# Two ScalarE steps' scores in one visit to TensorE's row mode, an eighth pooled PSUM bank, and stage rules dropped, in an attention and feed-forward kernel

## The chip, the cores and the metric

The kernel runs on one core of one Trainium2 chip. The metric is the device time of one execution in microseconds (us); the span in a profile is some 1.8 us shorter (703.6 us for a run of 705.39). The core's engines are called here by the profile's names: PE is TensorE (PEld its weight loads), ACT is ScalarE, DVE is VectorE, POOL is GpSimd, SP is SyncE, which issues DMAs. The kernel's PSUM tile, `ps`, has eight banks; a bank holds one 128 x 512 tile in float32.

## The reference, cut to what matters

```
xn  = layernorm(x)                       # x: 2048 x 640
q   = xn @ wq  -> 32 heads of 20         # k, v: one head of 20 for all
p   = softmax(q k^T / sqrt(20))          # 32 x 2048 x 2048 scores
att = (p v) @ wo
ffn = relu(xn @ w1 + b1)**2 @ w2 + b2    # 640 -> 1536 -> 640
out = x + att + ffn
```

The scores are the bulk: 2048 tiles of 128 x 512, each of which needs an exponential.

## The kernel before

The program is not written down instruction by instruction. A list scheduler inside the kernel runs at build time: it keeps a clock for each engine and always takes next the operation that can start first, with priorities for ties. The order in which it takes them is the program. The parts that the change touches are these.

ACT takes two or three score tiles at a time from adjacent PSUM banks (a *step*). TensorE makes a score tile with 20 contracted rows, so four heads sit in four row tiles of the array; nearly everything else it does here uses column tiles of 32 columns.

```
def make_act(st_):
    n, s0, b0 = len(st_["tiles"]), st_["s0"], st_["banks"][0]
    ...
    return Op(f"ACT{st_['j']}", "ACT", 0.05 + 0.4267 * n, [... func=AF.Exp, bias=-EXP_SHIFT, scale=SCALE ...], deps)
```

DVE and POOL make the other exponentials in sets of four tiles from integer operations: DVE takes each score tile out of PSUM (`tmore<-ps`), then DVE or POOL makes three more passes over the set. When a step's scores are issued, free row tiles are filled with score tiles for DVE:

```
elif kind == "qk":
    take_step(ap[1])
    heads = [t[2] for t in ap[1]["tiles"]]
    while len(heads) < HPG:
        r = make_dqk(heads)            # a tile for DVE, if a bank is free
        ...
```

The product with V (called PV) of one block of queries accumulates in a bank of its own, number 7, over 16 key tiles, and is then copied out by DVE. The other seven banks form a pool for ACT's steps, DVE's tiles and the feed-forward and projection groups. Finally, the scheduler has some twenty parameters, and a table that changes them by *stage* (a stage is 10 us of ACT's time):

```
NB = 7            # pooled banks
PVB = 7           # PV's bank
RULES = {3: {'PVA': 2.1, 'PVD': 2.1, 'R3': 1, 'PP': 0.9},
         4: {'PVA': 2.1, 'PVD': 2.1, 'R3': 1, 'PP': 0.9, 'WARM': 0.78},
         ...                           # 70 stages in all, many with none
         69: {'R3': 0, 'JIT': 1.1}}
```

The softmax here doesn't subtract the row's maximum and nothing guards it: scores larger than these inputs give would overflow.

Of the kernel before, what the change touches and what calls it, by code (L numbers as in the profile page):

```python
# [25 lines left out]
EPS = 1e-5  # L26
# [9 lines left out]
def _pl(z):  # L36
# [9 lines left out]
NB = 7  # L46
PVB = 7
# [33 lines left out]
RULES = {3: {'PVA': 2.1, 'PVD': 2.1, 'R3': 1, 'PP': 0.9},  # L81
         4: {'PVA': 2.1, 'PVD': 2.1, 'R3': 1, 'PP': 0.9, 'WARM': 0.78},
         5: {'D1P': 1, 'MPRIO': 0.5, 'PBIAS': 2.5},
         6: {'D1P': 1, 'MPRIO': 0.5, 'PBIAS': 2.5, 'ND': 1, 'QKP': 0},
         7: {'DQP': 2.05, 'URG': 2, 'PVD': 2.1, 'BEHIND': -0.3},
         8: {'WARM': 0.85, 'DQP': 0.95},
         10: {'ND': 1, 'NOPEN': 3},
         11: {'ND': 1, 'NOPEN': 3},
         12: {'EPS': 0.12},
         13: {'EPS': 0.06, 'EVP': 0.3},  # L90
         15: {'PBIAS': 0},
         17: {'EPS': 0.06},
         18: {'EPS': 0.12},
         19: {'WARM': 0.78, 'PBIAS': 2.5, 'IDLE': 0.3},
         21: {'PBIAS': 0, 'KEEP': 0},
         23: {'EPS': 0.12},
         25: {'R3': 1, 'EVP': 0.3},
         26: {'R3': 1, 'EVP': 0.3, 'IDLE': 0.3, 'PVD': 2.1},
         28: {'EPS': 0.12, 'URG': 3},
         29: {'EPS': 0.12, 'URG': 3, 'KEEP': 3, 'EVP': 1.1, 'ND': 3},  # L100
         31: {'PBIAS': 1, 'D1P': 1, 'PVD': 1.05},
         32: {'PBIAS': 1, 'D1P': 1, 'PVD': 1.05, 'DGAP': 0.8, 'DQP': 0.95, 'SQP': 2, 'R3': 1},
         36: {'PP': 0.9, 'BEHIND': -0.1, 'EVP': 0.3, 'PBIAS': 1.5},
         37: {'URG': 3, 'JIT': 1.0, 'PVD': 1},
         38: {'SQP': 0.7, 'URG': 3},
         39: {'PP': 2.5},
         40: {'PBIAS': 1},
         41: {'PBIAS': 1, 'DGAP': 1.5, 'SQP': 0.7},
         42: {'PBIAS': 1, 'DGAP': 1.5, 'SQP': 2, 'NOPEN': 3, 'ND': 2, 'PVD': 1},
         43: {'PBIAS': 1, 'DGAP': 1.5, 'SQP': 2, 'NOPEN': 3, 'ND': 2, 'PVD': 1, 'R3': 9},  # L110
         44: {'WARM': 0.78, 'KEEP': 3, 'DLAST': 7.5},
         45: {'DGAP': 0.8, 'KEEP': 1, 'D1P': 3},
         48: {'PBIAS': 1},
         49: {'PBIAS': 1, 'R3': 1},
         50: {'PBIAS': 1, 'R3': 1},
         53: {'DLAST': 3.5},
         54: {'DLAST': 3.5, 'EPS': 0, 'EVP': 0.3},
         55: {'DLAST': 3.5, 'EPS': 0, 'EVP': 0.3, 'ND': 1},
         56: {'EVP': 2, 'MPRIO': 1.0},
         57: {'R3': 1, 'ND': 1},  # L120
         58: {'BEHIND': -0.1, 'EPS': 0, 'PP': 4, 'R3': 1},
         59: {'BEHIND': -0.1, 'EPS': 0, 'PP': 4, 'R3': 1, 'DRATE': 0.95, 'DLAST': 10, 'PVA': 2.1},
         60: {'EVP': 1.1},
         61: {'EVP': 1.1, 'SQP': 0.7},
         62: {'EVP': 1.1, 'SQP': 0.7, 'KEEP': 3, 'R3': 1, 'NOPEN': 2, 'D1P': 3},
         64: {'PP': 0.9, 'DRATE': 0.8},
         65: {'R3': 1},
         66: {'R3': 1},
         67: {'EPS': 0.12, 'PVA': 1.05},
         68: {'R3': 0},  # L130
         69: {'R3': 0, 'JIT': 1.1}}
HOOK = None
PRIO = {'NM15': 2.12, 'NM10': 2.88, 'PW2': 0.96}
NBEF = {'AG4': 10.21, 'NM7': 11.5, 'Qe0_1': 10.11, 'PW12': 25.33}
XACT = (1, 3)
QEACT = (0, 1, 2, 3)
STOP = None
WINDOW = 3.4
MPRIO = 0.9
BEHIND = 0.12  # L140
IDLE = 0.3
EARLY = 12
EARLYK = "F"
FFN0 = 0.3
OUT0 = 0.5
QLEAD = 3.0
PEND = NBLK - 3.0
QCPOS = 0
# [76 lines left out]
def bass_parallel_sum__grouped_kv_mqa__dense_activation_squared_relu__prompt_kernel(nc, A_x, A_wq, A_wk, A_wv, A_wo, B_x, B_w1, B_b1, B_w2, B_b2, out):  # L225
    es = ExitStack()
    with es:  # L227
# [694 lines left out]
        def make_pv(b, kt):  # L922
# [7 lines left out]
            if first and b > 0:  # L930
                deps.append(tn_op[b - 1])
# [527 lines left out]
```

## Time and profile before

| of the kernel before | |
|---|---|
| time, median of 4 runs | 705.88 us (705.3 to 706.61) |
| span; granted TensorE clock | 703.6 us; 1.00 |
| busy: PE, ACT, DVE, POOL | 99%, 98%, 92%, 61% |
| first exponential starts, last one ends | 15.30 us, 695.14 us |
| ACT's waits for PE in the exponentials | 3.8 us in 3 waits |

Read the table with the chain of waits, not with the busy shares. The chain lies on ACT's exponentials for 94% of the span, so the time is when the exponentials start, how much work they are, how long ACT stands still among them, and what follows the last. I use these four terms. All are read from the trace: the work is the count of steps times 0.490, 0.917 or 1.344 us for one, two or three tiles, and a stall is what lies between the ends of two successive steps beyond that price. Before, they are 15.30 + 677.0 + 2.7 + 8.50 = 703.5 us. The lines themselves stand in the prediction. Three words recur. The *ramp* is the start, up to about 40 us, the *tail* what follows the last exponential, and a *waiting step* is one whose scores must wait until the step just in front has been read, because it needs a bank of that step. In the lines, `PT<-ps` is an exponential of ACT, `ps<-qT,kT` scores, `tmore<-ps` a tile taken by DVE, `ps<-kT,zeros` filler matmuls whose result changes nothing, and `R<-drs` the small DMA that brings row sums.

### The profile page before, as it was taken

Reading aid. Unit: us, or ns where it says so; the run is one execution under the profiler, and the core shown is the slowest. Engines: PE = TensorE matmul, PEld = TensorE weight load, DVE = VectorE, ACT = ScalarE, POOL = GpSimd, SP = SyncE. Lnnn points to the kernel's source line nnn. Section 1 sums busy time; section 2 is a strip of 40 time slices with the busy share of each in tenths; the row PEclk is TensorE's granted clock in tenths of the full one; section 3 lists DMA queues with packets and bytes.
Section 4 is the critical chain, followed back from the end, with each engine's and each line's share of the span. In section 5 each row is a group of like instructions: output and inputs, shape, how many; then the busy total and the mean of one; then the engine's idle time right before and its main releaser. Section 6 shows DMA issues by size and latency. Waiting matters only on the chain.

```text
span 703.6 us, 22608 instructions
## 1 busy us (share of the span) xinstructions
PE 695.0 (99%) x9780; PEld 216.0 (31%) x9781; DVE 645.9 (92%) x1125; ACT 687.5 (98%) x739; POOL 427.3 (61%) x268
## 2 busy tenths in 40 slices
PE   8999999999999999999999999999999999999997
PEld 4422223233322223332322222323333222233333
DVE  7789999999999998989998998899899999999894
ACT  6899999999999999999999999999999999999995
POOL 4767556567566764666568765766665675644253
PEclk9999999999999999999999999999999999999999
DMA  6325422233337701211101001111112100031201
GB/s 201 98 70 153 115 78 58 81 97 80 84 85 160 162 20 25 55 40 37 52 18 40 23 22 28 29 47 26 46 42 51 36 22 23 20 106 51 55 26 39
DMA packets 42016, 44.00 MB, mean 63 GB/s; under 512 B 15540, under 2 KB 32772, under 8 KB 41788
## 3 DMA queue, kind: packets, MB, share of 16 engines
q1 hardware_dynamic: 39132, 36.93, 19.2%
q0 software_dynamic: 2208, 5.25, 3.9%
q8 instruction: 76, 1.25, 0.7%
q10 hardware_dynamic: 576, 0.38, 0.2%
q14 instruction: 24, 0.20, 0.1%
HBM read 28.03 MB, written 14.91 MB: 61 GB/s over the span
## 4 chain that ended last, share of the span: by engine, by line
ACT 95%; PE 4%; DMA 1%; DVE 0%; SPq 0%; issue 0%; DVEq 0%
ACT PT L910 94%; PE ps L367 3%; DMA x_sb<-in_A_x_dram 1%; PE ps L540 1%; ACT xnT L477 0%; ACT OC L421 0%; DVE out_sb L1164 0%; PE ps L568 0%; SPq L384 0%; ACT OC L422 0%; SPq L391 0%; PE ps L510 0%; PE ps L496 0%; DVEq L227 0%; DVE PT L1164 0%
## 5 line engine op out<-in xcount | busy, mean ns | idle before, releaser
L910 ACT ACTIVATE PT<-ps 128x1024 bf16<-128x1024 f32 (+1 forms) x715 | 677.1, 1219 | 3.8 <-PE ps L367 3.8
L1083 DVE TENSOR_SCALAR tmore<-ps 128x512 uint16<-128x512 f32 x568 | 367.4, 683 | 31.7 <-PE ps L367 28.2
L1101 POOL TENSOR_SCALAR tmore<-tmore 128x2048 uint16<-128x2048 uint16 x109 | 206.4, 1900 | 171.1 <-PE ps L367 62.3
L367 PE MATMUL ps<-qT,kT 20*128 20x512 bf16 x2048 | 281.7, 384 | 1.9 <-ACT PT L910 0.8
L1101 POOL TENSOR_SCALAR x_sb<-tmore 128x2048 uint16<-128x2048 uint16 x100 | 189.3, 1902 | 79.4 <-DVE x_sb L1101 24.2
L367 PEld LDWEIGHTS ps<-qT,kT 20*128 20x128 bf16 x2048 | 71.6, 91 | 280.4 <-ACT PT L910 233.1
L367 PE MATMUL ps<-PT,vx 128*32 128x512 bf16 x1480 | 136.9, 386 | 0.2 <-ACT PT L910 0.2
L1101 DVE TENSOR_SCALAR x_sb<-tmore 128x2048 uint16<-128x2048 uint16 x135 | 96.1, 745 | 0.1
L367 PE MATMUL ps<-x_sb,vxs 128*32 128x512 bf16 x940 | 83.2, 382 | 0.0
L367 PE MATMUL ps<-xnT,w_sb 128*32 128x512 bf16 x960 | 77.2, 384 | 0.1
L367 PE MATMUL ps<-w_sb,big 128*32 128x320 bf16 x1536 | 74.5, 302 | 0.0
L367 PE MATMUL ps<-tmore,vxs 128*32 128x512 bf16 x764 | 69.6, 382 | 0.0
L1101 DVE TENSOR_SCALAR tmore<-tmore 128x2048 uint16<-128x2048 uint16 x82 | 61.5, 770 | 0.1
L367 PE MATMUL ps<-tmore,vx 128*32 128x512 bf16 x568 | 55.7, 382 | 0.0
L367 PEld LDWEIGHTS ps<-PT,vx 128*32 128x32 bf16 x1480 | 34.9, 94 | 62.1 <-issue 53.6
L367 PEld LDWEIGHTS ps<-w_sb,big 128*32 128x32 bf16 x1536 | 32.1, 95 | 29.3 <-issue 22.2
L648 DVE TENSOR_SCALAR hT_tmp<-ps,b1col 128x512 bf16<-128x512 f32 x48 | 35.8, 746 | 3.4 <-PE ps L367 2.7
L367 PE MATMUL ps<-xnT,wq_sb 128*32 128x512 bf16 (+1 forms) x480 | 33.7, 356 | 0.2 <-DVE tmore L1083 0.2
L367 PE MATMUL ps<-wo_c,OC 128*32 128x320 bf16 x608 | 30.9, 301 | 0.0
L367 PEld LDWEIGHTS ps<-x_sb,vxs 128*32 128x32 bf16 x940 | 21.3, 95 | 19.9 <-issue 13.4
L367 PEld LDWEIGHTS ps<-xnT,w_sb 128*32 128x32 bf16 x960 | 17.6, 94 | 26.7 <-issue 22.4
L367 PEld LDWEIGHTS ps<-tmore,vxs 128*32 128x32 bf16 x764 | 18.1, 95 | 16.4 <-issue 11.5
(81 smaller groups left out, 259.4 us busy)
## 6 DMA issues: line engine op xcount, KB each, us to landing
xbd<-b2d SPq DMA_DIRECT2D x16, 320.0 KB, 4.4
xbd<-in_A_x_dram POOLq DMA_DIRECT2D x8, 640.0 KB, 5.8
xr<-xbd SPq DMA_DIRECT2D x32, 160.0 KB, 2.4
w_sb<-in_B_w_dram SPq DMA_DIRECT2D x8, 480.0 KB, 4.4
big<-OR SPq DMA_DIRECT2D x71, 40.0 KB
big<-drs SPq DMA_DIRECT2D x71, 40.0 KB
out_dram<-out_sb SPq DMA_DIRECT2D x15, 160.0 KB, 1.8
qT<-QCr SPq DMA_DIRECT2D x108, 20.0 KB
```

The costliest lines, as they stand in the source:

```text
L367: return lambda e: e.matmul(out_, l, r, start=start, stop=stop, tile_position=tp)
L540: return [(lambda e, dt=dt: e.transpose(out=psbf(bk)[:, dt * 128:(dt + 1) * 128], in_=xn_sb[:, st, dt:D:DT], identity=ident[:])) for dt in ...
L648: o = Op(f"RL{qc}_{f}", "DVE", 0.66, [lambda e: e.tensor_scalar(out=hT_tmp[:, k % 2, :], in0=ps[:, bk, :], scalar1=b1col[:, f:f + 1], scal ...
L910: return Op(f"ACT{st_['j']}", "ACT", 0.05 + 0.4267 * n, [lambda e: e.activation(out=PT[:, s0:s0 + n, :], in_=ps[:, b0:b0 + (n - 1) * db + ...
L1083: d1 = op(f"D1_{n}_{i}", "DVE", 0.60, lambda e: e.tensor_scalar(out=L[:, cs].bitcast(U16), in0=ps[:, bank, :], scalar1=XA, scalar2=XB, op0 ...
L1101: p = op(f"P{j}_{n}", eng, 0.60 if eng == "DVE" else 1.86, lambda e, T=T, j=j, two=two: e.tensor_scalar(out=T.bitcast(U16), in0=L.bitcast( ...
```

## The change

The intent is to spare TensorE some of its changes between row and column mode: if three pooled banks are still free after the scores of one step have been issued, the scores of the next step follow in the same visit. To have the banks, all eight are pooled, and PV takes whichever is free when a block begins. The table of rules is emptied, and a few settings change. `DJIT`, a new limit on how far ahead DVE's tiles are issued, plays no part: built with the limit at 99, the changed kernel is the same program.

```diff
-NB = 7
-PVB = 7
+NB = 8
+PV0 = 7
-RULES = {3: {'PVA': 2.1, 'PVD': 2.1, 'R3': 1, 'PP': 0.9},
- ... (70 stages)
+DJIT = 9.0
+DV = 3
+RULES = {}
-PRIO = {'NM15': 2.12, 'NM10': 2.88, 'PW2': 0.96}
-NBEF = {'AG4': 10.21, 'NM7': 11.5, 'Qe0_1': 10.11, 'PW12': 25.33}
+PRIO = {'XN1': 0.13}
+NBEF = {'S4a': 6.0, 'AG5': 10.23, 'PW1': 4.94}
-QEACT = (0, 1, 2, 3)
+QEACT = (0, 1)
-FFN0 = 0.3
+FFN0 = 0.6
 ... (ACTST and POOLXN: which engine does which row statistics)
+        def bank_for(b):
+            if b in pv_bank:
+                return pv_bank[b]
+            can = [(bank_state(bk), -bk) for bk in range(NB) if bank_state(bk) is not None and ...]
+            return -min(can)[1] if can else None
 ... (PV's matmuls and its copy use this bank; the copy frees it)
                 take_step(ap[1])
                 heads = [t[2] for t in ap[1]["tiles"]]
+                if len(heads) == 2 and ... sum(1 for bk in POOLED if bank_state(bk) is not None and bank_state(bk) <= o.start + 0.06) >= par("DV"):
+                    can = [bk for bk in range(NB - 1) if all(k != kept() and ... for k in (bk, bk + 1))]
+                    st_ = build_step(len(steps), [can[0], can[0] + 1], 0.0) if can else None
+                    ... (if its heads differ and it is ready: commit it, take it)
```

More of the change, by code (lines that the diff above doesn't have):

```diff
@@ L80 @@
 KEEP = 1
-RULES = {3: {'PVA': 2.1, 'PVD': 2.1, 'R3': 1, 'PP': 0.9},
-         4: {'PVA': 2.1, 'PVD': 2.1, 'R3': 1, 'PP': 0.9, 'WARM': 0.78},
-         5: {'D1P': 1, 'MPRIO': 0.5, 'PBIAS': 2.5},
-         6: {'D1P': 1, 'MPRIO': 0.5, 'PBIAS': 2.5, 'ND': 1, 'QKP': 0},
-         7: {'DQP': 2.05, 'URG': 2, 'PVD': 2.1, 'BEHIND': -0.3},
-         8: {'WARM': 0.85, 'DQP': 0.95},
-         10: {'ND': 1, 'NOPEN': 3},
-         11: {'ND': 1, 'NOPEN': 3},
-         12: {'EPS': 0.12},
-         13: {'EPS': 0.06, 'EVP': 0.3},
-         15: {'PBIAS': 0},
-         17: {'EPS': 0.06},
-         18: {'EPS': 0.12},
-         19: {'WARM': 0.78, 'PBIAS': 2.5, 'IDLE': 0.3},
-         21: {'PBIAS': 0, 'KEEP': 0},
-         23: {'EPS': 0.12},
-         25: {'R3': 1, 'EVP': 0.3},
-         26: {'R3': 1, 'EVP': 0.3, 'IDLE': 0.3, 'PVD': 2.1},
-         28: {'EPS': 0.12, 'URG': 3},
-         29: {'EPS': 0.12, 'URG': 3, 'KEEP': 3, 'EVP': 1.1, 'ND': 3},
-         31: {'PBIAS': 1, 'D1P': 1, 'PVD': 1.05},
-         32: {'PBIAS': 1, 'D1P': 1, 'PVD': 1.05, 'DGAP': 0.8, 'DQP': 0.95, 'SQP': 2, 'R3': 1},
-         36: {'PP': 0.9, 'BEHIND': -0.1, 'EVP': 0.3, 'PBIAS': 1.5},
-         37: {'URG': 3, 'JIT': 1.0, 'PVD': 1},
-         38: {'SQP': 0.7, 'URG': 3},
-         39: {'PP': 2.5},
-         40: {'PBIAS': 1},
-         41: {'PBIAS': 1, 'DGAP': 1.5, 'SQP': 0.7},
-         42: {'PBIAS': 1, 'DGAP': 1.5, 'SQP': 2, 'NOPEN': 3, 'ND': 2, 'PVD': 1},
-         43: {'PBIAS': 1, 'DGAP': 1.5, 'SQP': 2, 'NOPEN': 3, 'ND': 2, 'PVD': 1, 'R3': 9},
-         44: {'WARM': 0.78, 'KEEP': 3, 'DLAST': 7.5},
-         45: {'DGAP': 0.8, 'KEEP': 1, 'D1P': 3},
-         48: {'PBIAS': 1},
-         49: {'PBIAS': 1, 'R3': 1},
-         50: {'PBIAS': 1, 'R3': 1},
-         53: {'DLAST': 3.5},
-         54: {'DLAST': 3.5, 'EPS': 0, 'EVP': 0.3},
-         55: {'DLAST': 3.5, 'EPS': 0, 'EVP': 0.3, 'ND': 1},
-         56: {'EVP': 2, 'MPRIO': 1.0},
-         57: {'R3': 1, 'ND': 1},
-         58: {'BEHIND': -0.1, 'EPS': 0, 'PP': 4, 'R3': 1},
-         59: {'BEHIND': -0.1, 'EPS': 0, 'PP': 4, 'R3': 1, 'DRATE': 0.95, 'DLAST': 10, 'PVA': 2.1},
-         60: {'EVP': 1.1},
-         61: {'EVP': 1.1, 'SQP': 0.7},
-         62: {'EVP': 1.1, 'SQP': 0.7, 'KEEP': 3, 'R3': 1, 'NOPEN': 2, 'D1P': 3},
-         64: {'PP': 0.9, 'DRATE': 0.8},
-         65: {'R3': 1},
-         66: {'R3': 1},
-         67: {'EPS': 0.12, 'PVA': 1.05},
-         68: {'R3': 0},
-         69: {'R3': 0, 'JIT': 1.1}}
@@ L148 @@
 QCPOS = 0
-ACTST = (2, 5, 6)
-POOLXN = (2, 7, 9, 10, 11, 13, 14, 15)
+ACTST = (0, 2, 4)
+POOLXN = (7, 9, 10, 11, 13, 14, 15)
 ROWP = (-0.5, 0.6, 0.8, 1.2)
@@ L159 @@
 DEFAULTS = dict(EVP=EVP, PBIAS=PBIAS, MPRIO=MPRIO, DGAP=DGAP, DLAST=DLAST, DRATE=DRATE, BEHIND=BEHIND, IDLE=IDLE, URG=URG, NOPEN=NOPEN,
-                EPS=0.03, JIT=JIT, R3=R3, STATIC=STATIC, PVA=1, PVD=1, D1P=1, PP=4, SQP=2, DQP=3, QKP=0, ND=2, WARM=WARM, KEEP=KEEP)
+                EPS=0.03, JIT=JIT, R3=R3, STATIC=STATIC, PVA=1, PVD=1, D1P=1, PP=4, SQP=2, DQP=3, QKP=0, ND=2, WARM=WARM, KEEP=KEEP, DJIT=DJIT, DV=DV)
 class Ctr:
@@ L506, in fill_parts @@
         def fill_parts():
-            return [mm(ps[32 * jj:32 * jj + 32, PVB, :], zeros32[:, :], kT[:, 0:512], False, False, (0, 32 * jj)) for jj in range(4)]
+            return [mm(ps[32 * jj:32 * jj + 32, pv_bank[pv_blk[0]], :], zeros32[:, :], kT[:, 0:512], False, False, (0, 32 * jj)) for jj in range(4)]
         def warm_parts():
-            return [lambda e: e.matmul(ps[:, PVB, :], ones_bf[:, :], hT_tmp[:, 0, :], start=True, stop=True)]
+            return [lambda e: e.matmul(ps[:, PV0, :], ones_bf[:, :], hT_tmp[:, 0, :], start=True, stop=True)]
         def need_te(sts):
@@ L857, in make_step @@
             t0 = max(free["PE"], horizon() - par("JIT"))
-            st_of = {bk: bank_state(bk) for bk in range(NB)}
+            keep = kept()
+            st_of = {bk: bank_state(bk) if bk != keep else None for bk in range(NB)}
             ok = [bk for bk in range(NB) if st_of[bk] is not None and st_of[bk] <= t0 + 0.02]
@@ L920, in after_act, with kept, pv_begin @@
                     pv_ready[key[0]].append(("A", key[1]))
+        pv_bank = {0: PV0}
+        bank_busy[PV0] = True
+        def bank_for(b):
+            if b in pv_bank:
+                return pv_bank[b]
+            can = [(bank_state(bk), -bk) for bk in range(NB) if bank_state(bk) is not None and not (par("STATIC") and bk in HELD)]
+            return -min(can)[1] if can else None
+        def kept():
+            b = pv_blk[0]
+            return bank_for(b) if b < NBLK and b not in pv_begun else None
+        def pv_begin(b):
+            if b not in pv_begun:
+                pv_bank[b] = bank_for(b)
+                bank_busy[pv_bank[b]] = True
+                pv_begun.add(b)
         def make_pv(b, kt):
@@ L924, in make_pv @@
             parts, deps = [], []
+            bank = bank_for(b)
             for h in range(HPG):
@@ L927, in make_pv @@
                 deps.append(o)
-                parts.append(mm(ps[32 * h:32 * h + 32, PVB, :], vx[:, kt, :], PT[:, sl, :], first, last, (0, 32 * h)))
+                parts.append(mm(ps[32 * h:32 * h + 32, bank, :], vx[:, kt, :], PT[:, sl, :], first, last, (0, 32 * h)))
             deps.append(v_op[kt // 4])
-            if first and b > 0:
-                deps.append(tn_op[b - 1])
+            if first:
+                deps.append(bank_rel[bank])
             return Op(f"PV{b}_{kt}", "PE", 0.222, parts, deps)
@@ L939, in make_dpv @@
             parts = []
+            bank = bank_for(b)
             for h in range(HPG):
                 i = s["order"].index(h)
-                parts.append(mm(ps[32 * h:32 * h + 32, PVB, :], wgt[:, kt, :], src[:, i * 512:(i + 1) * 512], first, last, (0, 32 * h)))
+                parts.append(mm(ps[32 * h:32 * h + 32, bank, :], wgt[:, kt, :], src[:, i * 512:(i + 1) * 512], first, last, (0, 32 * h)))
             deps.append(v_op[kt // 4])
@@ L945, in make_dpv @@
                 deps.append(vs_op[kt // 4][term - 1])
-            if first and b > 0:
-                deps.append(tn_op[b - 1])
+            if first:
+                deps.append(bank_rel[bank])
             return Op(f"DPV{b}_{kt}_{term}", "PE", 0.2205, parts, deps)
@@ L966, in emit_norm @@
             a = b % NOR
+            pb = pv_bank[b]
             if b >= NBLK - 2:
                 Tn, T2 = OR[:, a, :], QCr[:, 0, :]
-                tn = op(f"TN{b}", "DVE", 0.63, lambda e: e.transpose(out=Tn, in_=ps[:, PVB, :]), [lastpv] + or_users[a], prio=0)
+                tn = op(f"TN{b}", "DVE", 0.63, lambda e: e.transpose(out=Tn, in_=ps[:, pb, :]), [lastpv] + or_users[a], prio=0)
+                tn.frees = pb
                 rc = op(f"RC{b}", "DVE", 0.155, lambda e: e.reciprocal(out=Tn[:, DH:512:32], in_=Tn[:, DH:512:32]), [tn], prio=0)
@@ L977, in emit_norm @@
                 return
-            tn = op(f"TN{b}", "DVE", 0.60, lambda e: e.tensor_copy(out=OR[:, a, :], in_=ps[:, PVB, :]), [lastpv] + or_users[a], prio=0)
+            tn = op(f"TN{b}", "DVE", 0.60, lambda e: e.tensor_copy(out=OR[:, a, :], in_=ps[:, pb, :]), [lastpv] + or_users[a], prio=0)
+            tn.frees = pb
             tn_op[b] = tn
@@ L1041, in pool_banks @@
         def pool_banks():
+            keep = kept()
             if par("STATIC"):
-                return [bk for bk in POOLED if bk not in HELD and bank_state(bk) is not None]
-            fb = [bk for bk in POOLED if bank_state(bk) is not None]
+                return [bk for bk in POOLED if bk not in HELD and bk != keep and bank_state(bk) is not None]
+            fb = [bk for bk in POOLED if bk != keep and bank_state(bk) is not None]
             return fb if len(fb) > par("KEEP") else []
@@ L1055, in make_dqk @@
             if not fb or (len(fb) == 1 and behind()):
+                return None
+            if max(free["DVE"], free["PE"]) + sum(o.dur for o in dve_q if o.frees is not None) > free["PE"] + 0.43 + par("DJIT"):
                 return None
@@ L1119, in tail_bank @@
             bs = [bk for bk in range(NB) if (bk not in HELD or done) and bank_state(bk) is not None]
-            if tn_op.get(NBLK - 1) is not None and tn_op[NBLK - 1].fin is not None and not bank_busy[PVB]:
-                bank_rel[PVB] = bank_rel[PVB] or tn_op[NBLK - 1]
-                bs.append(PVB)
             return min(bs, key=lambda bk: (bank_state(bk), bk)) if bs else None
@@ L1229, in bass_parallel_sum__grouped_kv_mqa__dense_activation_squared_relu__prompt_kernel @@
             b = pv_blk[0]
-            if b < NBLK and (b == 0 or b - 1 in tn_op):
+            if b < NBLK and (b == 0 or b - 1 in tn_op) and bank_for(b) is not None:
                 for k, (kind, x) in enumerate(pv_ready[b]):
@@ L1309, in bass_parallel_sum__grouped_kv_mqa__dense_activation_squared_relu__prompt_kernel @@
                 heads = [t[2] for t in ap[1]["tiles"]]
+                if len(heads) == 2 and not par("STATIC") and sum(1 for bk in POOLED if bank_state(bk) is not None and bank_state(bk) <= o.start + 0.06) >= par("DV"):
+                    can = [bk for bk in range(NB - 1) if all(k != kept() and bank_state(k) is not None and bank_state(k) <= o.start + 0.06 for k in (bk, bk + 1))]
+                    st_ = build_step(len(steps), [can[0], can[0] + 1], 0.0) if can else None
+                    if st_ is not None and len(st_["tiles"]) == 2 and not set(t[2] for t in st_["tiles"]) & set(heads):
+                        rd = st_["qk"].ready()
+                        if rd is not None and rd <= o.start + 0.06:
+                            st_["qk"].dur = 0.005
+                            commit(st_["qk"])
+                            st_["qk"].lat = 0.425
+                            take_step(st_)
+                            heads += [t[2] for t in st_["tiles"]]
                 while len(heads) < HPG:
@@ L1324, in bass_parallel_sum__grouped_kv_mqa__dense_activation_squared_relu__prompt_kernel @@
             elif kind == "pv":
-                pv_begun.add(ap[1])
+                pv_begin(ap[1])
                 pv_of[(ap[1], pv_ready[ap[1]].pop(ap[2])[1])] = o
@@ L1328, in bass_parallel_sum__grouped_kv_mqa__dense_activation_squared_relu__prompt_kernel @@
             elif kind == "dpv":
-                pv_begun.add(ap[1])
+                pv_begin(ap[1])
                 s_, term = ap[3], ap[4]
```

## The prediction

> **What bounds the kernel now.** I read the page's first and fourth parts, then the chain in order of time, then the groups kept apart by shape, then TensorE's own timeline. First the busy shares and the chain of the kernel before:
>
> ```profile
> PE 695.0 (99%) x9780; PEld 216.0 (31%) x9781; DVE 645.9 (92%) x1125; ACT 687.5 (98%) x739; POOL 427.3 (61%) x268
> ...
> ACT 95%; PE 4%; DMA 1%; DVE 0%; SPq 0%; issue 0%; DVEq 0%
> ```
>
> TensorE (PE) and ScalarE (ACT) both look full. The chain in order of time (start, us, what) decides between them:
>
> ```profile
> 32.07 0.35 PE ps L367 x3
> 32.42 0.02 issue
> 32.44 661.79 ACT PT L910 x699
> 694.23 0.04 issue
> 694.27 3.90 PE ps L367 x104
> ```
>
> From 32.44 to 694.23 us the end is set by the exponentials on ACT alone. In the table of 10 us stretches ACT is 10.00 busy in every one from 40 to 690. Before 32 us TensorE sets the pace, and after 694.23 us 9.4 us of output projection follow. ACT's own waits are short:
>
> ```profile
> ACT PT L910 <- PE ps L367: 3.8, 3, 2.3
> ```
>
> 3.8 us in three waits, all before 32.44. So the time is nearly (start of the exponentials, 15.3) + (ACT's work) + (stalls, 2.8) + (8.5 from the last exponential to the end). The groups by shape give ACT's work:
>
> ```profile
> L910 ACT ACTIVATE PT<-ps 128x1024 bf16<-128x1024 f32 x665 | 621.9, 1190 | 1.4 <-PE ps L367 1.4
> L910 ACT ACTIVATE PT<-ps 128x1536 bf16<-128x1536 f32 x50 | 79.0, 1609 | 2.3 <-PE ps L367 2.3
> ```
>
> The 1190 ns of one overlap the next. Taking the trace's ends, a step of two score tiles ends 0.917 us after the one before, a step of three 1.344 us (medians). So a tile costs 0.427 us and a step 0.063 us on top; 665 x 0.917 + 50 x 1.344 = 677.0 us, the page's 677.1 for the group. There are 2048 tiles: 665 x 2 + 50 x 3 = 1480 go to ACT, 568 to VectorE (DVE), which builds exp from integer passes, four tiles to a set.
>
> TensorE has little slack beneath that. Its timeline (start, length):
>
> ```profile
> 310.40 0.40 PE L367 MATMUL ps<-PT,vx 128*32 128x512 bf16 x4
> 310.62 0.39 PE L367 MATMUL ps<-tmore,vx 128*32 128x512 bf16 x4
> 310.95 0.39 PE L367 MATMUL ps<-qT,kT 20*128 20x512 bf16 x4
> 311.27 0.62 PE L367 MATMUL ps<-tmore,vxs 128*32 128x512 bf16 x8
> ```
>
> A group of four 512-wide column tiles takes 0.22 us to the next group; but going to the scores (row tiles) takes 0.33, and from them 0.32 whether two, three or four are issued. A visit to the row mode thus costs about 0.32 + 0.105 = 0.426 us. With 714 runs of scores in the program's order that is 304 us; adding every group of column tiles at 0.22 (0.138 for 320 columns) gives 675 us of TensorE work, against 677 us for ACT.
>
> **What the Trainium skill says.** "ScalarE: Activation LUTs", section What ACT_TABLE_LOAD costs, gives 0.833 ns per element and a fixed part per ACTIVATE of which some overlaps; 512 x 0.833 = 427 ns, exactly the trace's slope, while the exposed fixed part here is 63 ns, which no figure there gives. "Perfetto Trace Analysis", section Identifying the Most-Contended Engine, warns that matmul busy share is no measure for TensorE; the trace agrees, since at 99% its weight loads still waited 238.9 us for ACT. "TensorEngine Tiling (Array Packing)", section Gotcha 1: PSUM Pressure, says that row tiles need different PSUM banks and that row tiling raises the pressure on them; this is the resource I expect to matter. I found no page with a price for changing between row and column tiles; the 0.105 us is the trace's.
>
> **The change part by part.** It does three things. (a) It lets two ACT steps' scores go out in one visit if, after the first, three pooled banks are free. (b) It puts the eighth bank into the pool; the bank that accumulates PV is now any free bank and moves from block to block. (c) It drops the 70 stage rules to which the scheduler had been tuned and changes small settings (which engine does which row statistics, three priorities). Because a scheduler decides the order, I counted the built programs.
>
> Work of ACT: 723 steps of two, 15 of three, one of one: 739 steps, 1492 tiles, against 715 and 1480. By the prices above 723 x 0.917 + 15 x 1.344 + 0.49 = 683.7 us, 6.6 more: 12 tiles are 5.1 us (three DVE sets fewer, 139 for 142) and 24 steps are 1.5. Two of four small evictions of q leave ACT (0.28 us each), before the exponentials begin. ACT is the chain, so the 6.6 us go into the time whole.
>
> Work of TensorE: only 24 visits carry two ACT steps and one carries three; the runs of scores are 715 against 714, since the steps are more numerous. So TensorE's work is 673, against 675: part (a) as such saves almost nothing. There are 52 groups of filler against 3; the 49 more, 10.8 us at 0.22, occupy only idle time. DVE loses 12 evictions (683 ns) and 16 passes, POOL gains 7 passes (1900 ns); both beside other work.
>
> Stalls of ACT: here is my main cost. In the order I followed, for each ACT step, which earlier ACT step its score matmul waits for (it needs that step's bank). Before, this is the step two back, or three, in all but two cases (steps 0 and 15, the latter being the 2.35 us wait in the trace), so ACT always has a filled pair of banks while TensorE fills the next. After, 15 steps wait for the step directly in front: 0, 8, 16 and 23 in the ramp and 127, 128, 358, 377-379, 607-611 later. There the two engines alternate. In the trace, scores start at the soonest 0.05 us after the ACT step they waited for, and where ACT waits it starts 0.435 us after the scores; an ACT step not overlapped lasts 1.017. So such a step takes 0.05 + 0.435 + 1.017 = 1.50 us in place of 0.917, a stall of 0.585 or more. Where TensorE has more work than that between the two scores (1.75 at 377, 378 and 379), it is that work less 0.917. Less some 0.36 us of lead: 127-129 come to 2.5 us, 358 to 0.7, 377-380 to 2.5, 607-611 to 3.2, others 0.2: 9.1 us. Why there: these steps stand mostly where a PV block ends; the finished accumulator waits for its copy, the new one has taken another bank, DVE's tiles hold two or three, and only one adjacent pair is left.
>
> The ramp: by the same sums of TensorE work over ACT work, steps 0 to 23 stall 2.7 us (2.8 before). The first score comes after 4.47 us of TensorE work in place of 5.07, so I start the exponentials at 14.3 in place of 15.3 (the trace cannot show this; say +-0.7).
>
> Sum: 14.3 + 683.7 + 2.7 + 9.1 + 8.5 (the tail's instructions are the same) = 718.3 us of span; the measured time was 705.39 for a span of 703.6, so +1.8: about 720 us, or +2.1%.
>
> **The rivals.** 1: The bank stalls are smaller, as the freed row-mode time and pairs let ACT run ahead; for it speaks that 25 visits prefill two steps. Then only ACT's extra work counts: 703.6 + 6.6 - 1 + 1.8 = 711. Against: the waiting steps are in the program's order, no lead survives them. 2: TensorE becomes the bound, as its work exceeds ACT's in some stretches and the untuned order also waits for DVE and POOL results, which the counts do not show; for it the 52 fillers, against it that the average load fell. That could add another 5: 725. 3: It is faster, since switches are saved. That needs ACT to do less, and it does more; the ramp can give 2 or 3 us at most, so below 705 is nearly excluded.
>
> **Range and chances.** ACT's 683.7 with start and tail gives a floor near 709 with no stall. The stalls are an estimate of 12 us with an uncertainty of some 4 either way and more room above. I take 720, with 715 to 726 for 8 in 10. The 2% line lies at 719.5, inside that range and close to its centre: 0.52 slower, 0.47 within 2%, 0.01 faster.
>
> **What would show it.** Right: the exponentials' group has x723 and x15 with about 684 us busy; ACT's waits for PE rise from 3.8 us in 3 to about 12 us in some 15 waits, most of 0.4 to 1.7 us, clustered near a sixth, a half and four fifths of the run; 10 us stretches with ACT near 8 there; the chain passes from ACT to PE at those places; the tail stays near 9 us. Wrong: ACT's waits stay under 5 us (then about 712), or rise above 20 with other releasers (DVE, POOL), or the first exponential starts well off 14.3.

## The result

The changed kernel is slower. Its two fast runs took 723.15 and 722.72 us; two further runs were slow, 748.85 and 754.71 us, at a granted clock of 0.963 and 0.952. The ratio of fast runs is 1.0241 (95% interval 1.0216 to 1.0266); here and below a ratio is the mean time of one kernel's fast runs over that of the other's of the same rounds, so it is not quite the ratio of the medians quoted. The kernel before had no slow run. Until the section on the slow runs, only fast runs are compared.

The page of the changed kernel, first and fourth part (busy us, share of the span and instructions by engine; then the chain that ended last):

```profile
PE 709.2 (98%) x9945; PEld 222.4 (31%) x9945; DVE 645.0 (89%) x1100; ACT 695.7 (96%) x761; POOL 440.6 (61%) x274
...
ACT 67%; PE 30%; DVE 1%; DMA 0%; issue 0%; POOL 0%; DVEq 0%
```

ACT's busy time rose by 8.2 us, and still its share fell, because the span grew by more. The chain, 95% on ACT before, now lies on PE for 30%. That does not say that PE has 30% more to do. In order of time (start, length, what):

```profile
39.77 72.05 ACT PT L863 x78
111.82 0.05 issue
111.86 23.32 PE ps L319 x338
135.18 0.03 issue
135.21 5.60 PE ps L319 x109
140.83 60.12 ACT PT L863 x65
```

At 140.83 an ACT step waited for its scores, so the chain goes over to PE there and runs back along PE's own queue, as far as the last place where PE waited for ACT (111.8). One stall puts a long piece on PE's account. The exponentials by shape:

```profile
L863 ACT ACTIVATE PT<-ps 128x1024 bf16<-128x1024 f32 x723 | 668.2, 1168 | 11.0 <-PE ps L319 10.7
L863 ACT ACTIVATE PT<-ps 128x1536 bf16<-128x1536 f32 x15 | 23.5, 1570 | 3.3 <-PE ps L319 3.3
```

Idle before them is 11.0 + 3.3 us, against 1.4 + 2.3 before. All but 0.3 us of it was ended by PE. The list of waits (total, times, longest) has the same and one line that matters later:

```profile
ACT PT L863 <- PE ps L319: 14.0, 21, 2.0
...
DVE R L961 <- DMA R<-drs: 1.6, 1, 1.6
```

ACT's timeline shows what such stalls look like (start, busy, count, and in brackets the idle time before and what ended it):

```profile
367.10 3.92 ACT L863 ACTIVATE PT<-ps 128x1024 bf16<-128x1024 f32 x4
371.57 1.02 ACT L863 ACTIVATE PT<-ps 128x1024 bf16<-128x1024 f32 x1 [0.55 <-PE ps L319]
373.30 1.03 ACT L863 ACTIVATE PT<-ps 128x1024 bf16<-128x1024 f32 x1 [0.71 <-PE ps L319]
375.04 5.80 ACT L863 ACTIVATE PT<-ps 128x1024 bf16<-128x1024 f32 x6 [0.71 <-PE ps L319]
```

The starts are 1.73 us apart, where two-tile steps are otherwise 0.92 apart. These are steps 377 to 379, counted from 0. In the program, 376 to 379 all take their scores from banks 2 and 3, so each must wait until the one in front has been read, and only then can PE begin.

The four terms, from the traces:

| | start | ACT's work | stalls | tail | sum |
|---|---|---|---|---|---|
| before | 15.30 | 677.0 | 2.7 | 8.50 | 703.5 |
| changed | 14.64 | 683.6 | 14.5 | 8.54 | 721.3 |
| difference | -0.7 | +6.6 | +11.8 | 0.0 | +17.8 |

### The profile page after: what moved, and what is told of

It is laid out like the page before. It is cut to its first block, busy times and chain, and to the rows that moved or that the text cites. A ratio compares the mean times of both kernels' runs of the same rounds, so it can differ in the third digit from the quotient of the medians.

```text
span 721.4 us, 22894 instructions
## 1 busy us (share of the span) xinstructions
PE 709.2 (98%) x9945; PEld 222.4 (31%) x9945; DVE 645.0 (89%) x1100; ACT 695.7 (96%) x761; POOL 440.6 (61%) x274
## 4 chain that ended last, share of the span: by engine, by line
ACT 67%; PE 30%; DVE 1%; DMA 0%; issue 0%; POOL 0%; DVEq 0%
ACT PT L863 67%; PE ps L319 29%; PE ps L492 1%; DMA x_sb<-in_A_x_dram 0%; PE ps L462 0%; DVE tmore L1065 0%; PE ps L520 0%; DVE out_sb L1143 0%; PE ps L427 0%; DVE x_sb L1083 0%; DVE xnT L495 0%; PE ps L448 0%; DVE OR L378 0%; DVE OR L379 0%; POOL rstd L386 0%
## 5 line engine op out<-in xcount | busy, mean ns | idle before, releaser
L863 ACT ACTIVATE PT<-ps 128x1024 bf16<-128x1024 f32 (+1 forms) x739 | 686.0, 1176 | 14.2 <-PE ps L319 14.0
L1065 DVE TENSOR_SCALAR tmore<-ps 128x512 uint16<-128x512 f32 x556 | 359.6, 682 | 40.7 <-PE ps L319 37.3
L1083 POOL TENSOR_SCALAR tmore<-tmore 128x2048 uint16<-128x2048 uint16 x115 | 218.0, 1905 | 147.8 <-DVE x_sb L1083 57.1
L319 PE MATMUL ps<-qT,kT 20*128 20x512 bf16 x2048 | 285.7, 384 | 5.9 <-ACT PT L863 4.6
L319 PE MATMUL ps<-PT,vx 128*32 128x512 bf16 x1492 | 140.1, 386 | 0.6 <-ACT PT L863 0.6
L1083 DVE TENSOR_SCALAR x_sb<-tmore 128x2048 uint16<-128x2048 uint16 x129 | 101.6, 811 | 0.1
L1083 DVE TENSOR_SCALAR tmore<-tmore 128x2048 uint16<-128x2048 uint16 x72 | 54.5, 772 | 0.0
L319 PEld LDWEIGHTS ps<-x_sb,vxs 128*32 128x32 bf16 x920 | 22.4, 95 | 20.5 <-issue 14.3
L608 DVE TENSOR_TENSOR big<-hT_tmp 128x512 bf16<-128x512 bf16 x48 | 27.4, 588 | 0.0
```

Source lines behind the costliest of these rows:

```text
L319: return lambda e: e.matmul(out_, l, r, start=start, stop=stop, tile_position=tp)
L608: q = op(f"SQ{qc}_{f}", "DVE", 0.34, lambda e: e.tensor_tensor(out=h2T[:, f, :], in0=hT_tmp[:, k % 2, :], in1=hT_tmp[:, k % 2, :], op=ALU. ...
L863: return Op(f"ACT{st_['j']}", "ACT", 0.05 + 0.4267 * n, [lambda e: e.activation(out=PT[:, s0:s0 + n, :], in_=ps[:, b0:b0 + (n - 1) * db + ...
L1065: d1 = op(f"D1_{n}_{i}", "DVE", 0.60, lambda e: e.tensor_scalar(out=L[:, cs].bitcast(U16), in0=ps[:, bank, :], scalar1=XA, scalar2=XB, op0 ...
L1083: p = op(f"P{j}_{n}", eng, 0.60 if eng == "DVE" else 1.86, lambda e, T=T, j=j, two=two: e.tensor_scalar(out=T.bitcast(U16), in0=L.bitcast( ...
```

## The experiments

Theory: the loss is ACT's extra work and its bank stalls, and both come from an order that is no longer tuned; the double visits themselves do little. Rivals: the double visits cost it (two steps take four of seven banks); the roaming PV bank costs it; or TensorE's load, not the banks, makes the stalls. In each experiment the line numbers of a kernel's file shift a little, so the exponentials stand at another line.

### Rules dropped, and nothing else (e1_norules)

```diff
-RULES = {3: {...}, ..., 69: {...}}
+RULES = {}
```

The edit is made to the kernel before.

> The kernel before with its 70 stage rules dropped and nothing else. Counted in the built program: 731 steps of ACT with 1488 tiles, so 681.4 us of work against 677.0, and no later step that waits for the step in front of it (0 and 15 only, as before). My theory, that most of the loss is the loss of the tuning: about 714 us (712 to 717), half or more of the 17 us. Rival 'double visits': within 1% of before (below 712). Rival 'roaming bank': the same, below 712.

Measured: 718.03 us (717.43 to 719.76), ratio 1.0179 (1.0162 to 1.0196). This alone is 12 of the 17 us, above the range that I gave. The terms are 14.88 + 681.4 + 7.8 + 12.49: work +4.4 us, stalls +5.0, and a tail that is 4.0 us longer, which I had not counted. The waits of ACT in this run, with the evacuation in the tail that waited longest:

```profile
ACT PT L860 <- PE ps L317: 8.0, 9, 1.9
ACT xr L1111 <- PE ps L317: 4.9, 1, 4.9
```

The order without rules leaves PE more to do after the last exponential. No step after the ramp waits for the step in front of it here. At steps 357 and 470 (0.4 and 1.9 us) PE worked on without a gap, so there it had more work than ACT. The stalls of steps 652 to 655 (2.7 us together) go with something else, a fall of the granted clock (window, length, busy time of PE, PEld, DVE, ACT and POOL, granted clock, DMA share, GB/s):

```profile
624.00:628.00 4.00, 3.58 (x23) 0.59 (x22) 4.00 (x7) 3.41 (x4) 1.73 (x1) 0.58 0.24 57
628.00:632.00 4.00, 4.00 (x52) 1.34 (x50) 1.43 (x3) 2.28 (x3) 1.90 (x1) 0.57 0.30 64
```

All four runs had a clock of 0.993 to 0.998, so part of the 12 us is likely the clock's. The rest says that the rules bought work, stalls and tail alike. Neither new mechanism is in this kernel, so neither rival can be the whole loss.

### The small settings as well (e2_settings)

```diff
 RULES = {}
-PRIO = {'NM15': 2.12, 'NM10': 2.88, 'PW2': 0.96}
+PRIO = {'XN1': 0.13}
 ... (NBEF, QEACT, FFN0, ACTST, POOLXN as in the changed kernel)
```

> The kernel before without rules and with the small settings of the changed one (row statistics, q evictions, three priorities, start of the feed-forward part); neither the double visits nor the eighth bank in the pool. Counted: 738 steps, 1492 tiles, 683.6 us of work, waiting steps 8, 16 and 24 in the ramp only. My theory: 715 to 719 us, 1 to 4 us over the run without rules. Rivals 'double visits' and 'roaming bank': below 712, as the loss would still be to come.

Measured: 719.66 us (719.12 to 722.17), ratio 1.0205 (1.0185 to 1.0225): 1.6 us more than without rules, within the 1 to 4 us expected; the time itself is 0.7 us above the range given. The terms are 15.17 + 683.6 + 7.8 + 11.36. All of the 6.6 us of extra ACT work is there already, without the code for double visits.

### The changed kernel without double visits (e3_no_double)

```diff
-DV = 3
+DV = 99
```

> The changed kernel with the double visits switched off and all else kept. Counted: 737 steps, 1492 tiles, 683.5 us of work, and 10 later steps that wait for the step in front (61, 313 to 315, 336, 338, 339, 516, 517, 608), 11 in the changed kernel. My theory: double visits are nearly nothing, 719 to 724 us, ACT's waits for PE 12 to 15 us. Rival 'double visits': below 714.

Measured: 721.32 us (720.98 to 721.68), ratio 1.0221 (1.0206 to 1.0237). The terms are 15.12 + 683.5 + 12.6 + 8.54.

```profile
ACT PT L863 <- PE ps L319: 12.7, 18, 2.0
```

Switching the double visits off brings 1.6 us, at 721.3 for 722.9, and not the loss. Of the 25 visits in the changed kernel that carry scores for two or more steps, 7 exist here too, because two visits happened to stand next to each other. Between these two orders, e2 and e3, the roaming bank costs 4.8 us of stalls and saves 2.8 us of tail.

### PV in a fixed bank again, double visits kept (e4_fixed_bank)

```diff
-NB = 8
+NB = 7
         def bank_for(b):
-            if b in pv_bank:
-                return pv_bank[b]
+            return PV0 if b == 0 or b in pv_begun or not bank_busy[PV0] else None
```

> The changed kernel with PV in the fixed bank 7 again (seven banks in the pool), the double visits kept. Counted: 746 steps, 1508 tiles, 690.9 us of work (four DVE sets fewer than in the changed kernel), one later step (109) that waits for the step in front. My theory: the stalls in the steady part go (ACT's waits for PE 4 to 6 us, in the ramp), but 7 us more work take their place: 717 to 723 us. Rival 'roaming bank' (its stalls are the whole loss): below 714.

Measured: 721.04 us (719.94 to 721.85), ratio 1.0221 (1.0204 to 1.0238). The terms are 14.48 + 690.9 + 4.2 + 8.54.

```profile
ACT PT L863 <- PE ps L319: 5.6, 6, 2.0
```

Here the bank stalls are gone: one later step (109) waits, 0.67 us. But four more DVE sets have gone over to ACT, 7.3 us of work, and the time moves by less than 2 us. In these two orders, want of bank room shows itself in two ways: as ACT standing still, or as tiles that DVE could not take. With e4 all four combinations of the two mechanisms have run without rules: neither (e2) 719.7 us, the roaming bank (e3) 721.3, double visits (e4) 721.0, both 722.9. (With its double visits off, e4's kernel builds e2's program but for the bank of one group in the tail.)

### The price of one waiting step (e5_onepair)

```diff
             t0 = max(free["PE"], horizon() - par("JIT"))
+            if stage[0] in ONEPAIR:                    # (30, 31)
+                if bank_state(0) is None or bank_state(1) is None:
+                    return None
+                return build_step(j, [0, 1], t0)
```

The base is the kernel of e1; in the two stages DVE's tiles may not use banks 0 and 1. The wait is made by the choice of banks, so the program is free of races.

> The price of a step that waits for the step in front, by itself: the kernel before without rules, in which ACT's scores may use only banks 0 and 1 (and nothing else may) for two of the 70 stages of the scheduler, so that the 12 steps 297 to 308 each need the banks of the step just before. My theory: in that stretch the ACT steps end 1.50 us apart or a little more (stall of 0.58 to 0.85 us each, 7 to 10 us together), whatever TensorE has to do. Rival 'TensorE's load': they end 0.92 to 1.1 us apart, since TensorE's own work per step (0.87 to 1.1 us) hardly exceeds ACT's.

Measured: one run, 719.43 us, state unknown, clock 0.999, so only the stretch is read. ACT's timeline there:

```profile
297.50 1.02 ACT L865 ACTIVATE PT<-ps 128x1024 bf16<-128x1024 f32 x1 [0.66 <-PE ps L318]
299.16 1.02 ACT L865 ACTIVATE PT<-ps 128x1024 bf16<-128x1024 f32 x1 [0.64 <-PE ps L318]
300.87 1.02 ACT L865 ACTIVATE PT<-ps 128x1024 bf16<-128x1024 f32 x1 [0.68 <-PE ps L318]
302.53 1.02 ACT L865 ACTIVATE PT<-ps 128x1024 bf16<-128x1024 f32 x1 [0.64 <-PE ps L318]
304.35 1.02 ACT L865 ACTIVATE PT<-ps 128x1024 bf16<-128x1024 f32 x1 [0.80 <-PE ps L318]
```

The starts are 1.66 to 1.82 us apart. The stalls of the 12 steps are 0.66 to 0.90 us each, 9.4 us in all, inside the 7 to 10 expected. PE's load per step, which the rival took for the limit, would have left ACT at 0.9 to 1.1 us. That a step waits for the step in front is enough.

### More banks kept free (e6_keep3)

```diff
-KEEP = 1
+KEEP = 3
```

> The changed kernel, in which DVE's tiles and the feed-forward groups may take a pooled bank only when more than three are free (one in the changed kernel). Counted: 747 steps, 1508 tiles, 691.0 us of work, and no later step that waits for the step in front. My theory (banks make the stalls, and they trade against DVE's tiles): steady stalls under 1 us in place of 11, work 7.4 us more, so 718 to 722 us. Rival 'TensorE's load makes the stalls': ACT's waits stay near 11 us in the steady part, about 729.

Measured: 727.02 to 740.34 us over four runs, at clocks of 0.975 to 0.993; three of them count as fast, and their ratio is 1.0374 (1.031 to 1.0437). The number missed. In the profiled run (734.01 us, clock 0.981) there are only the ramp's stalls and those of one stretch, steps 196 to 213, 14.3 us; the waiting steps of the changed kernel are gone (127, 128, 358, 377 to 379, 607 to 611), as the theory said. ACT's work is 691.0 us as counted. What came in their place was not foreseen. The same run by stretches (window, length, busy time of each engine, granted clock, DMA share, GB/s):

```profile
192.00:196.00 4.00, 4.00 (x56) 0.95 (x44) 4.00 (x7) 4.00 (x6) 0.96 (x1) 1.00 1.06 214
196.00:200.00 4.00, 2.21 (x29) 0.54 (x26) 0.58 (x3) 3.42 (x4) 1.76 (x2) 1.00 1.09 260
200.00:204.00 4.00, 3.31 (x31) 0.75 (x31) 3.48 (x7) 1.40 (x2) 3.16 (x2) 0.71 1.05 218
204.00:208.00 4.00, 4.00 (x32) 0.59 (x24) 2.33 (x4) 2.69 (x3) 0.59 (x1) 0.50 0.29 68
```

The engines in order are PE, PEld, DVE, ACT, POOL. The DMA share is over 1; DVE goes from 4.00 to 0.58; PE follows, at 2.21; then the clock goes to 0.50 and stays there to about 229 us, and ACT falls behind with it. This is taken up under the slow runs.

### The changed kernel again (e7_after_again)

No edit.

> The changed kernel once more, on the chip of these runs, because two of its four runs were slow at a granted clock of 0.95 to 0.96. Fast runs 722 to 724 us. If the slow state comes from the kernel, it shows again in some of the four; if from that chip at that time, not.

Measured: 727.39 and 724.11 us fast (clock 0.995 and 1.000), 744.43 and 747.57 slow (0.970, 0.966); ratio of the fast 1.0277 (1.0249 to 1.0305). One fast run is 3.4 us above the 722 to 724 expected; its trace has two stretches at half the clock, shown below. The slow state came back in two of four, and the kernel before, run beside it, had none in seven. Slow runs of one version or another are on three chips (5, 6 and 9), so it is not one chip's.

### Double visits in the tuned kernel (e8_double_alone)

```diff
 ... (the kernel before, its rules, its settings, PV in bank 7)
+DV = 3
+ ... (the double-visit block of the change)
```

> The kernel before with its rules, its settings and PV's fixed bank, and the double visits alone added. Counted: 735 steps, 1508 tiles, 690.2 us of work against 677.0, no later step that waits for the step in front. My theory: the visits save next to no TensorE work, and the rules, tuned to another order, no longer fit: seven DVE sets are lost, 13 us more work, and stalls somewhat above before: 718 to 726 us. Rival 'double visits gain where the kernel is tuned': at or below 705.

Measured: 726.34 us (725.29 to 728.68), ratio 1.028 (1.0263 to 1.0297), no slow run. The terms are 15.93 + 690.2 + 12.0 + 8.54. The time is just above the 718 to 726 expected. The profiled run was the slowest of the four: its clock was at 0.50 from 686 to 694 us, and 3.3 us of the 12.0 of stalls stand about there (steps 709 to 714); the longest, 4.3 us at step 703, comes before it. But the fastest run, 725.29 us at a clock of 1.000, is still slower than the changed kernel's. It is not evidence that a double visit is bad: the rules that it keeps were fitted to an order that no longer exists, and seven DVE sets fell away. It suggests that the mechanism cannot be judged without tuning the rules to it; that the misfit of the rules is the cause is argued, not shown.

### A constant that has nothing to do with the change (e9_warm)

```diff
-WARM = 0.72
+WARM = 0.85
```

> The changed kernel with one constant of the scheduler altered that has nothing to do with the change: it adds filler matmuls when TensorE's busy share in a 3.4 us stretch would fall under 0.85 instead of 0.72. Counted: 741 steps, 1492 tiles, 683.8 us of work, 23 visits with two steps, so the same work as the changed kernel, but only two later steps (219 and 632) that wait for the step in front, against 11. My theory (start + work + stalls + tail; the stalls are chance of the untuned order, not a property of the double visits): ACT's steady stalls 2 to 5 us, 713 to 718 us in fast runs. Rival 'the double visits themselves cost' : 722 to 724 as before. For the clock: if fillers hold it, no slow run; if the late reciprocal load is what breaks it, fillers do not help where the scheduler foresaw no wait.

Measured: 715.1 us (714.65 to 715.85), ratio 1.0139 (1.0122 to 1.0156), clock 0.999 or more in all four. The terms are 14.35 + 683.8 + 6.3 + 8.61, so nearly the same work as the changed kernel, the same roaming bank, 23 double visits, and 8.2 us fewer stalls. (The constant rules filler matmuls, but there are fewer of them, 188 for 208.) Whether steps are caught waiting for the step in front is an accident of the order. This also sets the scale for e2, e3 and e4: each is one order, and their differences of 1 to 2 us are smaller than the 8 us by which an unrelated constant moved the time. What they exclude is that either mechanism makes the whole loss. The orders without rules, with or without the new mechanisms (e1, e2, e3, e4, e9, e10, e11 and the changed kernel; e6 and the repeat e7, whose clocks were disturbed, aside), lie between 715 and 724 us in fast runs, all above the 706 of the tuned one.

### More margin for the small DMAs (e10_margin)

```diff
-DMARG = 4
+DMARG = 6
```

> The changed kernel with 6 in place of 4 us of margin that the scheduler adds to the landing of its small DMAs, so that DVE takes the reciprocal of the row sums later. Counted: 742 steps, 1500 tiles, 687.2 us of work, four later steps that wait for the step in front (81, 197, 519, 566). My theory of the slow runs (DVE stands in line for the row sums while the DMA engines are full, TensorE runs dry, its clock halves): no wait of DVE for that DMA, granted clock 0.995 or more in all four runs, and 717 to 721 us. Rival (the slow state is the chip's): slow runs at a clock of 0.95 to 0.97 come as often as in the changed kernel, 4 of 8.

Measured: 722.49, 723.05 and 723.68 us fast (clock 0.997), 739.31 slow (0.972); ratio 1.025 (1.0233 to 1.0267). The remedy failed, and the expectation with it: DVE still waited 3.4 us once for the row sums, near 200 us, and steps 198 and 199 stalled 2.15 and 2.12 us. As an experiment on the cause it decides nothing, since it did not remove the wait.

### The burst of loads spread out (e11_burst)

```diff
-            xb=[f"RL0_{k}" for k in range(6)] + ["RL3_3", "RL3_5"])
+            xb=["RL0_0", "RL0_6", "RL1_0", "RL1_6", "RL2_0", "RL2_6", "RL3_3", "RL3_5"])
```

Each name is the feed-forward operation after which one load of x into the residual may be issued.

> The changed kernel with four of the eight loads that add x into the residual in DRAM held back from the second block of the feed-forward part, where six follow each other closely, to later ones; the program's order is the changed kernel's up to about 190 us and differs after it. Counted: 737 steps, 1488 tiles, 681.8 us of work, five later steps that wait for the step in front (127, 128, 332, 628, 695). My theory of the slow runs (those loads fill the DMA engines near 200 us, the small DMA of the row sums lands late, DVE waits in line, TensorE runs dry and its clock halves): no wait of DVE for that DMA near 200 us, DMA share there under 0.8, granted clock 0.995 or more in all four runs, about 714 to 719 us. Rival (the slow state is not of this cause): a slow run at 0.95 to 0.97 in one or two of four.

Measured: 715.18 us (715.0 to 715.21), ratio 1.0137 (1.012 to 1.0154), clock 1.000 in all four. Steps 127 to 129 stall as in the changed kernel (2.2 us, the order is the same up to there). The stretch at 195 us in the changed kernel and then here, columns as above:

```profile
195.00:200.00 5.00, 4.98 (x65) 1.30 (x64) 3.56 (x6) 5.00 (x7) 4.39 (x3) 1.00 1.12 261
```

```profile
195.00:200.00 5.00, 5.00 (x66) 1.20 (x59) 5.00 (x10) 5.00 (x7) 2.24 (x2) 1.00 0.32 96
...
DVE R L961 <- DMA R<-drs: 0.3, 1, 0.3
```

The DMA share there is 0.32 for 1.12, DVE is busy throughout, and its one wait for the row sums is 0.3 us. The share is still 0.89 in the 5 us before, so "under 0.8 near 200" holds only after 195. Some of the gain against the changed kernel is again a luckier later order (1488 tiles, five later waiting steps).

### Rules for the changed kernel (e12_tuned)

```diff
-RULES = {}
+RULES = {1: {'DGAP': 0.8, 'KEEP': 1, 'D1P': 3},
+         ... (48 stages, among them 'DV': 2 or 3 by stage)
```

> The changed kernel with stage rules of its own: 48 of them, found by an hour's search with the kernel's own scheduler, which also chooses by stage whether double visits are allowed. Counted: 734 steps, 1492 tiles, 683.3 us of work, one later step (174) that waits for the step in front. My theory (the changed kernel lost chiefly by the missing rules): ACT's stalls 4 to 7 us in place of 14.5, 710 to 714 us, over half of the loss that is not ACT's extra work recovered. Rival (double visits and the roaming bank cost by themselves): still above 718. It is not expected to beat the kernel before, as its work alone is 6.3 us more.

Measured: 712.84 us; three fast runs at 712.38 to 712.87, one slow at 725.36 (clock 0.983); ratio 1.0102 (1.0085 to 1.0119). The terms are 14.81 + 683.3 + 4.3 + 8.53.

```profile
ACT PT L910 <- PE ps L366: 5.7, 6, 2.0
```

An hour of search brought back 10 of the 17 us with both mechanisms in place. What one constant did by chance (e9) was 8, so the 10 us are not a clean price of rules. The stalls are 1.5 us above those of before; the rest of what is left is 6.3 us of ACT work. I also let the same search start from the kernel before, with its rules and with double visits allowed by stage. It found no order that the scheduler itself held better by more than 0.01 us, so no such version was run, and none here beats the kernel before. That second search is a report and not a result.

### The slow runs

This concerns the changed kernel's slow state and not the 2.4% above. One chain in the traces of the fast runs is this. From 177 to 216 us in the changed kernel six loads of x into the residual follow each other; at 195 to 200 us the DMA share is 1.12. The small DMA that brings the row sums for a block's normalisation lands late, 8.9 us after its issue. DVE takes its operations in order and stands in line for it (1.6 us), so banks are not emptied and PE runs dry. In the repeat of the changed kernel (e7, clock 0.995) PE's timeline has the gap:

```profile
200.32 0.39 PE L319 MATMUL ps<-PT,vx 128*32 128x512 bf16 x4
202.30 0.61 PE L319 MATMUL ps<-qT,kT 20*128 20x512 bf16 x3 [1.59 <-DVE tmore L1065]
```

and the stretches of the same run show the clock fall right behind it:

```profile
198.00:202.00 4.00, 2.71 (x36) 0.65 (x32) 1.65 (x4) 3.48 (x4) 4.00 (x3) 1.00 1.08 237
202.00:206.00 4.00, 3.70 (x29) 0.76 (x29) 3.41 (x6) 2.05 (x2) 2.87 (x2) 0.57 0.33 75
206.00:210.00 4.00, 4.00 (x57) 1.09 (x54) 2.74 (x5) 3.82 (x5) 0.15 (x1) 1.00 0.23 56
```

A mean of 0.57 over 4 us is about 3.4 us at half the clock, and ACT is busy 2.05 of 4.00. In e6 the same beginning led to some 27 us at 0.50.

That is not the only way in. The waiting steps 607 to 611 make a gap in PE of their own, and in the same run of e7 the clock fell behind it too, so that step 611 stalled 2.3 us in place of 0.8 (PE's timeline, then the stretch):

```profile
594.50 0.39 PE L319 MATMUL ps<-qT,kT 20*128 20x512 bf16 x2 [1.12 <-ACT PT L863]
...
596.00:600.00 4.00, 4.00 (x38) 0.96 (x30) 3.73 (x7) 1.85 (x2) 1.50 (x2) 0.72 0.80 276
```

The changed kernel's first trace has the same gap of 1.12 us (at 590.65) and kept 1.00. In e1 and e8 the clock fell with no gap in PE of over 0.6 us after the ramp. Across kernels, DVE's wait for the row sums goes with slow runs:

| kernel | DVE's wait in the profile, us | slow runs |
|---|---|---|
| before | 0.5 | none |
| changed, and again (e7) | 1.6; 2.7 | 2 of 4; 2 of 4 |
| e6; e10 | 3.4; 3.4 | 1 of 4 each |
| e12; e9 | 0.9; 1.1 | 1 of 4; 0 of 4 |
| e11 (burst spread) | 0.3 | 0 of 4 |
| e1, e2, e3, e4, e8 | none listed | 0 of 20 |

That a gap precedes the fall of the clock is shown in e6 and e7, and e11 shows that with the burst spread the gap near 200 us is not there and four runs keep the clock. But e11's later order has no steps 607 to 611 that wait either, so it took both gaps away and does not tell which mattered; the kernel before has the same six loads in a row (204 to 244 us) and no slow run; and e12 and e9 stand in the table the wrong way round. No slow run has a trace of its own, so that their further 13 to 32 us are longer episodes of the same kind is argued, not shown; and four runs in e11 are few against a rate of four in eight.

## Why the prediction was right

The forecast was 720 us and slower at even odds; 722.9 came. By its own steps:

- **What bounds the kernel.** Right. The price of 0.917 and 1.344 us for a step gave 683.6 us of work, and the trace has the 723 steps of two, 15 of three and one of one that were counted. (The floor without stalls comes to 708.3 by the forecast's own terms, where it wrote 709.)
- **The stalls, where.** Right. All eleven later steps that were listed stalled in the trace, as did 8, 16 and 23. The minimum of 0.585 us is met within a few hundredths where PE was idle (0.59 at 609 and 610), and e5 confirmed it as a mechanism of its own.
- **The stalls, how much.** Under-sized. The sum given was 2.7 us in the ramp and 9.1 later; measured were 3.6 and 11.1 (stalls over 0.1 us alone, which is 0.2 more than the table's 14.5). By place, forecast and measured: 127 to 129, 2.5 and 2.2; 358, 0.7 and 0.7; 377 to 380, 2.5 and 2.5; 607 to 611, 3.2 and 3.5. The term that was off is "others 0.2": it was 2.3. These are steps 194 and 195 (0.8 together), where DVE's wait for the row sums kept the banks, and 266, 473 and 719 (0.4 to 0.7 each). Rival 2 named waits for DVE that the counts do not show; that is what happened at 194, and it is also the start of the slow runs, which the prediction did not see at all.
- **The start.** 14.3 forecast, 14.64 measured, inside the doubt given; the same program started at 15.18 in e7, so a miss of 0.3 us means nothing. **The tail.** 8.5 and 8.54. With +0.3, +0.9 and +2.0 the sum of 720.1 becomes 723.3, against the 722.9 measured.
- **Where the stalls come from.** Half right. The prediction put the waiting steps at the ends of PV blocks, and the trace agrees: DVE copies PV out at 135.8, 352.1, 370.5 and 586.2 us, and the four places begin to stall at 139.0, 353.1, 371.6 and 587.4. With PV's bank fixed (e4) they nearly vanish. But e9 keeps the roaming bank and has two of them, so the bank makes them possible, and the untuned order decides.
- **The double visits.** Right that they save almost nothing: TensorE's work, fillers aside, is the same to 2 us by count, and switching them off (e3) moves 1.6 us, within what a change of order does anyway.
- **Part (c), the rules.** Named as part of the change, but with no price of its own. It turned out to be the main one: 12 us alone (e1, some of it likely the clock's), and no order without rules had a median under 715 us. The forecast found the loss by counting the built program, so it could be right about the time without saying which part was to blame.

## What to carry to other kernels

When a kernel's order is made by a scheduler with a table of tuned exceptions, a new mechanism and the loss of the table must be priced apart: build the old kernel without the table first, and move one unrelated constant to learn how far an order wanders by chance. Once the order of a program is known, its bottleneck engine can be read from it: count its work, and mark every step whose buffer is still held by the step just in front of it. A late small DMA at the head of an in-order queue can cost far more than its wait if TensorE runs dry and loses its clock behind it: in e6 DVE's wait was 3.4 us, and the stalls that followed 14.3.

## What the Trainium skill lacked or had wrong

- "TensorE: Matmul & The Clock Gate", section Why this matters for your kernels, warns of PE gaps of more than about 3 us between bursts. In the trace of e7 the clock was at 0.57 in the 4 us that follow a single gap of 1.59 us, and in e6 at 0.71 and then 0.50 after one of 2.27 us; the 0.80 us gap in the changed kernel's fast run left it at 1.00, and one of 1.12 us was followed by 0.72 in e7 and by 1.00 in that fast run. Before the gaps of 1.59 and 2.27 us PE was issuing at its usual density. In e1 it fell to 0.58 with no gap of over 0.6 us, so the length of one gap does not decide it.
- "TensorEngine Tiling (Array Packing)" gives no price for changing between row tiles and column tiles. Here a 512-wide group of four column tiles takes 0.22 us to the next such group, 0.32 to a row group, and a row group 0.32 to the next column group, so about 0.1 us for each change.
- "ScalarE: Activation LUTs", section What ACT_TABLE_LOAD costs, has the slope right (0.833 ns an element; 427 ns a tile in the trace). The fixed part that shows between back-to-back exponentials read from PSUM is 63 ns here; the page's 186 ns (scale and bias immediate, as they are here) less 93 of overlap would be 93.
- No page that I read prices the round between two engines that share one buffer. Here scores start at the soonest 0.05 us after the ACT step that held their bank, and ACT starts 0.435 us after the scores; with nothing to overlap, a step takes 1.50 us in place of 0.917.
